# Convolution matmuls of one array half laid between the other half's layer-1 matmuls, and a softmax with its maximum

## The chip, the cores and the metric

The kernel runs on one NeuronCore of a Trainium2 chip. TensorE (PE) multiplies, with a weight load (PEld) in front of each matmul; its results go to PSUM. ScalarE (ACT) and VectorE (DVE) take results out of PSUM, GpSimd (POOL) casts and copies in SBUF, and SyncE (SP) issues nearly all DMAs. The metric is the device time of one execution in microseconds; less is better.

## The reference

`x` is 8 sequences of 4160 tokens with 192 features; `weight` is 8 heads by 7 taps.

```python
w = weight - np.max(weight, axis=-1, keepdims=True)
w = np.exp(w)
w = w / (np.sum(w, axis=-1, keepdims=True) + 1e-09)      # softmax over the 7 taps
x_pad = zeros of 6 rows in front of each sequence, then x
y[b, s, h, g] = sum over k of w[h, k] * x_pad[b, s + k, h, g]   # 24 features per head
h = np.maximum(np.maximum(y @ w1, y @ w2), y @ w3)       # 192 -> 768
out = h @ w_out                                          # 768 -> 192
```

So it is a causal convolution over seven tokens with one filter per head, followed by a feed-forward layer whose hidden value is the largest of three products.

## The kernel before, in words

**Blocks.** The 33280 tokens are cut into 65 blocks of 512 (`NB` is 65). The first four are convolved in a "dense" form (`conv_dense`, L363). The others have their tokens in 32-token pieces on both halves of the partitions and are convolved by `conv` (L341): one block alone, then four pairs, and from block 13 on (`QUADS`) thirteen groups of four. A group of four is convolved in two bursts of four heads each, in the two blocks t = u-4 and t = u-3 before its first block u, where `late` is true. There are thus 26 bursts of four heads.

**The maximum of three.** max(y w1, y w2, y w3) is computed as y w3 + max(relu(y(w1-w3)), y(w2-w3)); `wd` holds the differences, `m16` holds w3 w_out. In each block and for each of six slices j of 128 hidden units, `l1` (L491) makes two sums, `lp` and `lq`, each of three matmuls with 512 columns. `top` (L483) then lets ACT write r = relu(lp) and DVE write h = max(r, lq). `st2` (L533) multiplies h of the block before with `wo` (30 matmuls of 192 columns per half and block, named `po`), and `total` lets ACT and DVE add the halves' sums.

**Two lanes.** Contractions are 64 rows long, so each matmul uses one half of the 128 x 128 array, as a tile of 64 rows by 128 columns: lane 0 is the upper half (`lp`), lane 1 the lower half (`lq`). `mm` (L450) puts a matmul with its column count in a lane's queue, `op` (L454) puts work of other engines behind what was put so far, and `emit` (L461) writes the program: it always takes the next matmul from the lane whose `clock`, the sum of columns so far, is lower. `meet` (L477) empties both lanes and sets the clocks to zero.

**A burst.** In a late block, after `l1(t, 1)` and part of `st2`, `meet()` is called, and then `conv` writes 32 matmuls for four heads (line L354): for each head and each of four 32-token pieces j one on each half, with weights `band` of 39 rows by 32 columns. They are tiles of 64 x 32, so up to eight of them have places of their own in the array (two halves, four column groups). They fill four PSUM tiles G0 to G3, G0 and G2 on the upper half, G1 and G3 on the lower. `evac` (L388) casts them to `ys`, G0 and G2 on ACT, G1 and G3 on DVE. After the second burst `turn` (L398) issues the transposing DMAs from `ys` to `yp` on SP, and `load_on` (L736) issues further loads of `x`. After that the loop goes on with `st2` and `l1(t, 2)`.

**PSUM.** The pool `psp` has two buffers, used in turn by `lp` and G1; `psq` has two, used in turn by `lq` and G3; `psw` has four, for `po`, G0 and G2. A buffer can be written again once its reader (for `lp` the relu, for `lq` the max, for G the cast) is done.

**Start.** The filter's softmax is computed on eight partitions: `Exp` with a running sum on ACT, a reciprocal and a product on DVE (L265 to L271). From its result 38 small matmuls and copies make `band`.

Of the kernel before, what the change touches and what calls it, by code (L numbers as in the profile page):

```python
# [10 lines left out]
FP32 = mybir.dt.float32  # L11
FP16 = mybir.dt.float16
AXX = mybir.AxisListType.X
AF = mybir.ActivationFunctionType

P = 128
KW = 7
PAD = KW - 1
NHEAD = 8
GRP = 24  # L20
# [3 lines left out]
HALF = P // 2  # L24
# [4 lines left out]
def kernel(  # L29
# [12 lines left out]
    nc = tc.nc  # L42
# [15 lines left out]
    for b in range(B):  # L58
        s = nfull * NBLK
        while s < SEQ:  # L60
            n = min(SEQ - s, NBLK - off)
# [27 lines left out]
    TOK = 32  # L89
    NR = NBLK // TOK // 2  # L90
    LAP = PAD + 1
    KR = TOK + LAP
# [6 lines left out]
    const = ctx.enter_context(tc.tile_pool(name="const", bufs=1))  # L99
# [14 lines left out]
    QUADS = 13  # L114
# [58 lines left out]
    for t in range(NDENSE + 1, NB):  # L173
        u = (t - NDENSE - 1) % 2 if t < QUADS else (t - QUADS) % 4
        pairs[t] = (t - u, u, 2 if t < QUADS else 4)

    def place(t):
        return pairs.get(t, (t, 0, 0))

    x16s, slots = {}, {}  # L180
# [48 lines left out]
    wk = const.tile([NHEAD, KW], FP32)  # L229
# [18 lines left out]
    def keep_warm(n, pool=psw, tag="w"):  # L248

        ps = pool.tile([P, NBLK], FP32, tag=tag, name="idle")  # L250
        for _ in range(n):
            nc.tensor.matmul(ps[:], lhsT=idle[:, 0:P], rhs=idle[:], start=True, stop=True)
# [5 lines left out]
    line = const.tile([NHEAD, WIN + 31], FP16)  # L258
# [3 lines left out]
    band = const.tile([P, NHEAD, BAND_W], FP16)  # L262
    nc.vector.memset(band[:], 0.0)
    keep_warm(5, psp, "p")
    wexp = const.tile([NHEAD, KW], FP32)  # L265
    wsum = const.tile([NHEAD, 1], FP32)
    nc.scalar.activation(out=wexp[:], in_=wk[:], func=AF.Exp, accum_out=wsum[:])
    wrec = const.tile([NHEAD, 1], FP32)
    nc.vector.reciprocal(out=wrec[:], in_=wsum[:])
    zero_x(4)  # L270
    nc.vector.tensor_scalar_mul(out=line[:, 31:31 + KW], in0=wexp[:], scalar1=wrec[:])  # L271
    for v in range(2):
        nc.vector.memset(xz[1][v][:], 0.0)
    cast_dense(0, (nc.vector.tensor_copy, nc.vector.tensor_copy))
# [1 line left out]
    for lo, hi, copy in ((0, CUT, nc.scalar.copy), (CUT, WIN, nc.vector.tensor_copy)):  # L276
        bps = psq.tile([32, hi - lo + 3, NHEAD], FP32, tag="q", name=f"band_{lo}")
        for c in range(lo, hi):

            nc.tensor.matmul(bps[:, c - lo:c - lo + 4, :].rearrange("p c h -> p (c h)"),  # L280
                             lhsT=line[:, WIN - 1 - c:WIN + 31 - c],
                             rhs=ident16[0:NHEAD, 0:4 * NHEAD], start=True, stop=True)
        for a in range(4):
            copy(out=band[32 * a:32 * a + 32, :, 32 * a + lo:32 * a + hi],
                 in_=bps[:, 0:hi - lo, :].rearrange("p c h -> p h c"))
# [53 lines left out]
    dense, hs, outs, halves, convs, done = {}, {}, {}, {}, {}, {}  # L339

    def conv(t, pools, heads=range(NHEAD)):  # L341
        if t >= NB:
            return
        t0, _, nu = place(t)
        n = len(pools)
        per = len(heads) * 2 // n
        w = nu * 2 * GRP
        G = [pool.tile([P, per, w], FP32, tag=tag, name=f"G{i}_{t}_{heads[0]}")
             for i, (pool, tag) in enumerate(pools)]
        for k, h in enumerate(heads):  # L350
            for j in range(4):
                for i in range(2):
                    row = slice(HALF * i, HALF * i + KR)
                    nc.tensor.matmul(  # L354
                        G[2 * (k // per) + i][TOK * j:TOK * (j + 1), k % per, :],
                        lhsT=band[row, h, HALF * i + LAP:HALF * i + KR],
                        rhs=x16s[t0][row, h, j, :, :, :].rearrange("p u r c -> p (u r c)"),
                        start=True, stop=True, tile_position=(HALF * i, TOK * j))
        if heads[0] == 0:
            slots[t0] = ysp.tile([P, 2, nu, 2, D], FP16, tag="ys", name=f"ys_{t}")  # L360
        convs[t0] = G, heads[0]

    def conv_dense(t, copies, pools=((None, None),) * 2, order=(0, 1)):  # L363

# [23 lines left out]
    def evac(t, i, copy=nc.scalar.copy):  # L388
        if t >= NB:
            return  # L390
        G, h0 = convs[t]
        per = G[i].shape[1]
        h0 += per * (i // 2)
        copy(out=slots[t][:, i % 2, :, :, GRP * h0:GRP * (h0 + per)].rearrange(  # L394
                 "p u r (h c) -> p h (u r) c", c=GRP),
             in_=G[i][:].rearrange("p h (n c) -> p h n c", c=GRP))

    def turn(t, vs=(0,)):  # L398


        nu = place(t)[2]
        for v in vs:
            n = min(nu, 2)
            yp = ypp.tile([P, 2, 2, n, NC, P], FP16, tag="yp", name=f"yp_{t + v}")
            for u in range(n):
                dense[t + v + u] = yp
            for i in range(2):
                nc.sync.dma_start_transpose(out=yp[:, 0, i, :, :, :].rearrange("p u k n -> p (u k) n"),
                                            in_=slots[t][:, i, v:v + n, :, :].rearrange("p u r d -> p (u r d)"))
# [40 lines left out]
    def mm(i, cols, fn):  # L450
        lanes[i].append((cols, fn))
        put[i] += 1

    def op(fn):  # L454
        ops.append((tuple(put), fn))
# [5 lines left out]
    def emit(rest=False):  # L461


        run_ops()
        while lanes[0] or lanes[1]:
            i = 0 if clock[0] <= clock[1] else 1
            if not lanes[i]:
                if not rest:
                    return
                i = 1 - i  # L470
            cols, fn = lanes[i].popleft()
            fn()
            clock[i] += cols
            gone[i] += 1
            run_ops()
# [15 lines left out]
    def l1(t, j, pools=((psp, "p"), (psq, "q"))):  # L491


        ps = [None, None]

        def product(i, c, n):
            if n == 0:
                pool, tag = pools[i]
                ps[i] = pool.tile([P, NBLK], FP32, tag=tag, name=f"l{tag}{i}_{t}_{j}")
            nc.tensor.matmul(ps[i][:], lhsT=w_of(i, c, j),  # L500
                             rhs=y_all(t, i, c), start=(n == 0), stop=(n == NC - 1))

        for n in range(NC):
            for i in range(2):
                c = n if t >= NDENSE else (i, NC - 1, 1 - i)[n]
                mm(i, NBLK, lambda i=i, c=c, n=n: product(i, c, n))
        op(lambda: top(t, j, ps))
        emit()
# [162 lines left out]
    WPWQ = ((psw, "w"), (psp, "p"), (psw, "w"), (psq, "q"))  # L671
# [64 lines left out]
    def load_on(t):  # L736
        for v in range(loads[t - 1] + 1, loads[t] + 1):
            if v not in loaded:
                load_x(v)
# [4 lines left out]
    for t in range(2, NB):  # L744
        u = convs_at.get(t, NB)
        late = t > 2 and u < NB
        if t in (3, 4):
            double(t + 1)
        if t > 3:
            for v in range(casts.get(t - 1, 8) + 1, casts[t] + 1):  # L750
                cast_x(v)
        l1(t, 0)
        if t == 2:
            first_rest()
        elif t == 3:
            cast_x(8)
            nc.gpsimd.tensor_copy(out=m16[0:HALF, 2, :], in_=m16[HALF:P, 0, :])
            nc.gpsimd.tensor_copy(out=m16[HALF:P, 2, :], in_=m16[HALF:P, 1, :])
        if t > 3 and not late:
            op(lambda t=t: (store(t - 2, 0, 4, (nc.sync,)),  # L760
                            turn(t + 2, (2,)) if place(t + 2)[1:] == (0, 4) else None, load_on(t)))
        else:
            op(lambda t=t: store(t - 2, 0, 4, (nc.sync,)))
        cuts = ROOM if late else EVEN
        st2(t - 1, (cuts[0], cuts[0]))
        for j in range(1, NJ):
            l1(t, j)
            if late and j == 1:
                st2(t - 1, (cuts[0] + OWN + AHEAD, cuts[0] + OWN))
                meet()  # L770
                quad, second = u >= QUADS, u < QUADS or t == u - 3
                conv(u, WPWQ, range(4 * second, 4 * second + 4) if quad else range(NHEAD))
                for i in (0, 2):
                    evac(u, i)
                for i in (1, 3):
                    evac(u, i, nc.vector.tensor_copy)
                if second:
                    turn(u)
                load_on(t)
            if t == 2 and j == 1:  # L780
                meet()
                conv_dense(3, (ACT, DVE))
                zero_x(1, NQ, NR, nc.vector)
                cross(3, GP)
                load_x(8)
                cast_x(6)
            elif t == 2 and j == 3:
                meet()
                conv(u, WW)
                evac(u, 0)  # L790
                evac(u, 1, nc.vector.tensor_copy)
                turn(4)
                load_x(9)
                cast_x(7)
            st2(t - 1, (cuts[j], cuts[j]))
            if j == 1 and t > 4 and t + 2 in pairs and pairs[t + 2][1] % 2 == 0:
                double(t + 2)
            if t == NB - 1 and j == 3:
                op(lambda: store(NB - 2, 0, 2, (nc.sync,)))
        if t == NB - 1:  # L800
            op(lambda: store(NB - 2, 2, 4, (nc.sync,)))
# [29 lines left out]
```

## Time and profile before

| | |
|---|---|
| median of 3 runs | 454.51 us (454.46 to 455.02) |
| profiled execution, first to last instruction (span) | 452.8 us |
| the profiled execution's own time | not listed apart from its span; the median is 1.7 us above the span |
| TensorE busy / weight loads | 446.9 us (99%) / 411.5 us (91%) |
| DVE / ACT / POOL busy | 356.7 us (79%) / 320.0 us (71%) / 203.0 us (45%) |
| mean granted TensorE clock | 0.999 |
| chain that ended last | PE 96%, SP's queue 2%, DMA 1% |
| convolution matmuls (L354), 1152 of them | 17.3 us busy |
| casts of G (L394) | ACT 61, mean 482 ns; DVE 61, mean 550 ns |

In the profile an instruction group is named by line, engine, operation and out<-in. The start of a matmul is recorded; its end is modelled, so a matmul's listed length is longer than the time it holds the array, and the rate is read from the distance between starts. Times on the other engines are starts and lengths in us or ns.

### The profile page before, as it was taken

To read this page: it belongs to the slowest core of one execution; us is meant where nothing else is said; L and a number is where in the kernel's file an instruction comes from. 1 tells how busy PE (TensorE), PEld (TensorE's weight loads), DVE (VectorE), ACT (ScalarE), POOL (GpSimd) and SP (SyncE) were. 2 spreads that over 40 slices of the span, in tenths; PEclk is the share of its full clock that TensorE was granted. 3 is DMA by queue.
4 is the path that set the end of the run, shared out by engine and by line. 5 is a ranking of instruction groups with operands and counts; after the bars stand their busy time and mean duration, and the time that the engine had idled before them with its cause. 6 is when DMAs were issued, how large, how long until landed. Compare 5 with 4: busy or idle time off the path is not lost.

```text
span 452.8 us, 18491 instructions
## 1 busy us (share of the span) xinstructions
PE 446.9 (99%) x7702; PEld 411.5 (91%) x7702; DVE 356.7 (79%) x614; ACT 320.0 (71%) x605; POOL 203.0 (45%) x226
## 2 busy tenths in 40 slices
PE   8999999999999999999999999999999999999997
PEld 4569999999999999999999999999999999999996
DVE  7767778878878788887878788887878788787775
ACT  7767767767777676777767677776767777776664
POOL 2774836556454444635353363444346452504000
PEclk9999999999999999999999999999999999999999
DMA  7978977597966958497585958958594876435223
GB/s 205 231 186 152 225 188 196 143 202 184 171 177 141 178 127 225 123 175 183 119 189 143 192 137 161 199 137 182 135 213 115 178 189 119 116 88 104 59 72 106
DMA packets 127987, 72.03 MB, mean 159 GB/s; under 512 B 52064, under 2 KB 127711, under 8 KB 127903
## 3 DMA queue, kind: packets, MB, share of 16 engines
q1 hardware_dynamic: 127743, 70.75, 69.4%
q8 instruction: 60, 0.98, 1.0%
q14 instruction: 24, 0.20, 0.2%
q10 hardware_dynamic: 160, 0.10, 0.1%
HBM read 33.28 MB, written 25.56 MB: 130 GB/s over the span
## 4 chain that ended last, share of the span: by engine, by line
PE 96%; SPq 2%; DMA 1%; issue 0%; POOL 0%; DVE 0%; POOLq 0%
PE po L564 36%; PE lq L500 31%; PE lp L500 22%; PE G L354 3%; DMA ws<-in_moe_w_dram 1%; PE lw L523 1%; SPq L227 1%; SPq L223 1%; PE D L375 1%; PE po L622 0%; PE po L595 0%; PE lp L523 0%; SPq L164 0%; PE pm L334 0%; POOL wd L299 0%
## 5 line engine op out<-in xcount | busy, mean ns | idle before, releaser
L564 PE MATMUL po<-wo,h 64*128 64x192 f16 x3024 | 331.3, 243 | 0.7 <-issue 0.7
L488 DVE TENSOR_TENSOR h<-r,lq 128x512 f16<-128x512 f16 x384 | 263.0, 686 | 85.9 <-ACT r L487 78.2
L487 ACT ACTIVATE r<-lp 128x512 f16<-128x512 f32 x384 | 229.0, 597 | 115.1 <-PE lp L500 101.8
L500 PE MATMUL lp<-yp,wd 64*128 64x512 f16 x1098 | 295.7, 376 | 0.0
L500 PE MATMUL lq<-yp,wd 64*128 64x512 f16 x1098 | 295.5, 376 | 0.0
L564 PEld LDWEIGHTS <-h 64*128 64x128 f16 x3024 | 241.6, 94 | 6.8 <-issue 4.9
L500 PEld LDWEIGHTS <-wd 64*128 64x128 f16 x2268 | 179.1, 94 | 12.3 <-issue 0.2
L194 POOL CAST x<-xf 103x768 f16<-103x768 f32 x122 | 97.5, 827 | 107.5 <-DMA xf<-in_x_dram 82.0
L564 PE MATMUL po<-m,yp 64*128 64x192 f16 x720 | 141.1, 243 | 0.0
L417 POOL COPY yp<-yp 64x1536 f16<-64x1536 f16 (+1 forms) x62 | 89.6, 1445 | 95.9 <-DMA yp<-ys 70.6
L572 DVE TENSOR_TENSOR o<-a,po 128x384 f32<-128x384 f32 x126 | 69.0, 547 | 0.0
L564 PEld LDWEIGHTS <-yp 64*128 64x128 f16 x720 | 66.3, 94 | 0.3
L571 ACT COPY a<-po 128x384 f32<-128x384 f32 x126 | 59.5, 473 | 0.0
L394 ACT CAST ys<-G 128x384 f16<-128x384 f32 x61 | 26.3, 482 | 9.6 <-PE G L354 9.6
L394 DVE CAST ys<-G 128x384 f16<-128x384 f32 x61 | 31.0, 550 | 0.0
L354 PE MATMUL G<-x,band 39*32 39x192 f16 (+2 forms) x1152 | 17.3, 234 | 0.0
L354 PEld LDWEIGHTS <-band 39*32 39x32 f16 x1152 | 10.7, 91 | 5.2 <-issue 4.7
L500 PE MATMUL lp<-yd,wd 64*128 64x512 f16 x36 | 9.7, 376 | 0.0
L500 PE MATMUL lq<-yd,wd 64*128 64x512 f16 x36 | 9.7, 376 | 0.0
L211 POOL CAST xz<-xf 112x160 f16<-112x160 f32 (+2 forms) x15 | 4.4, 339 | 8.8 <-DVE w3s L303 7.6
L523 PEld LDWEIGHTS <-wd 128*128 128x128 f16 (+1 forms) x48 | 3.0, 96 | 5.6 <-issue 2.2
L375 PEld LDWEIGHTS <-xz 112*32 112x32 f16 x320 | 4.7, 107 | 3.3 <-POOL xz L211 1.3
(72 smaller groups left out, 97.6 us busy)
## 6 DMA issues: line engine op xcount, KB each, us to landing
xf<-in_x_dram SPq DMA_DIRECT2D x113, 234.0 KB
out_dram<-o SPq DMA_DIRECT2D x62, 384.0 KB
xf<-in_x_dram SPq DMA_DIRECT2D x7, 204.8 KB
xf<-in_x_dram SPq DMA_DIRECT2D x3, 420.0 KB
ws<-in_moe_w_dram SPq DMA_DIRECT2D x8, 128.0 KB
yp<-ys SPq DMA_TRANSPOSE x62
out_dram<-o SPq DMA_DIRECT2D x5, 192.0 KB
wos<-in_moe_w_out_dram SPq DMA_DIRECT2D x1, 576.0 KB
```

The costliest lines, as they stand in the source:

```text
L194: nc.gpsimd.tensor_copy(out=x16s[t0][0:K, :, :, u, r, :].rearrange("p h j c -> p j h c"), in_=xf[0:K, 4 * r:4 * r + 4, :].rearrange("p j ( ...
L354: nc.tensor.matmul(G[2 * (k // per) + i][TOK * j:TOK * (j + 1), k % per, :], lhsT=band[row, h, HALF * i + LAP:HALF * i + KR], rhs=x16s[t0] ...
L375: nc.tensor.matmul(ps[32 * g:32 * g + 32, lo:hi], lhsT=xz[t][v][0:rlen, q, 32 * s:32 * s + 32], rhs=band[0:rlen, h, cc:cc + hi - lo], star ...
L394: copy(out=slots[t][:, i % 2, :, :, GRP * h0:GRP * (h0 + per)].rearrange("p u r (h c) -> p h (u r) c", c=GRP), in_=G[i][:].rearrange("p h ...
L417: nc.gpsimd.tensor_copy(out=yp[HALF * i:HALF * (i + 1), 1, :, :, :, :].rearrange("p i u k n -> p (i u k n)"), in_=yp[HALF * (1 - i):HALF * ...
L487: nc.scalar.activation(out=r[:], in_=ps[0][:], func=AF.Relu)
L488: nc.vector.tensor_max(out=hs[t][:, j, :], in0=r[:], in1=ps[1][:])
L500: nc.tensor.matmul(ps[i][:], lhsT=w_of(i, c, j), rhs=y_all(t, i, c), start=(n == 0), stop=(n == NC - 1))
L523: nc.tensor.matmul(open_ps[t, j, i][:], lhsT=a, rhs=b, start=(t, j, i) not in begun, stop=(t, j, i) in begun)
L564: nc.tensor.matmul(ps[b0, i][:, s % 2, :], lhsT=a, rhs=b, start=first, stop=last)
L571: nc.scalar.copy(out=a[:], in_=ps[s - 1, 0][:])
L572: nc.vector.tensor_add(out=outs[t][:, s - 1:s + 1, :], in0=a[:], in1=ps[s - 1, 1][:])
```

## The change

The softmax subtracts the maximum of the seven taps (`reduce_max` with `negate`, given to `Exp` as a bias) and adds 1e-9 to the sum, by an eighth column that a `memset` fills; the sum is a `reduce_sum` on DVE in place of the running sum on ACT.

`conv` is split: `conv_parts` returns the matmuls as a list, and a G tile is taken from its pool when its first matmul is written. For the groups of four, the burst is replaced: after the same `meet()`, the 16 matmuls of the upper half go to lane 0, counted at 48 columns each, then the casts of G0 and G2, then all of `l1(t, 2)` in both lanes, and then the 16 matmuls of the lower half go to lane 1, then the casts of G1 and G3. `emit` mixes them by its clocks. `turn` and `load_on` stand behind these. The single block and the pairs keep their burst.

```diff
-    wexp = const.tile([NHEAD, KW], FP32)
-    wsum = const.tile([NHEAD, 1], FP32)
-    nc.scalar.activation(out=wexp[:], in_=wk[:], func=AF.Exp, accum_out=wsum[:])
+    wexp = const.tile([NHEAD, KW + 1], FP32)
+    nc.vector.memset(wexp[:], 1e-9)
+    wneg = const.tile([NHEAD, 1], FP32)
+    nc.vector.reduce_max(out=wneg[:], in_=wk[:], axis=AXX, negate=True)
+    nc.scalar.activation(out=wexp[:, 0:KW], in_=wk[:], func=AF.Exp, bias=wneg[:])
     wrec = const.tile([NHEAD, 1], FP32)
-    nc.vector.reciprocal(out=wrec[:], in_=wsum[:])
+    nc.vector.reduce_sum(out=wrec[:], in_=wexp[:], axis=AXX)
+    nc.vector.reciprocal(out=wrec[:], in_=wrec[:])
...
+        def product(k, h, j, i):
+            b = 2 * (k // per) + i
+            if G[b] is None:
+                pool, tag = pools[b]
+                G[b] = pool.tile([P, per, w], FP32, tag=tag, name=f"G{b}_{t}_{heads[0]}")
...
+        return [(i, j, lambda k=k, h=h, j=j, i=i: product(k, h, j, i))
+                for k, h in enumerate(heads) for j in range(4) for i in range(2)]
...
         for j in range(1, NJ):
-            l1(t, j)
+            if not (late and u >= QUADS and j == 2):
+                l1(t, j)
             if late and j == 1:
                 st2(t - 1, (cuts[0] + OWN + AHEAD, cuts[0] + OWN))
                 meet()
...
+                if quad:
+                    parts = conv_parts(u, WPWQ, heads)
+                    cols = place(u)[2] * 2 * GRP // 4
+                    for i in range(2):
+                        for a, _, fn in parts:
+                            if a == i:
+                                mm(i, cols, fn)
+                        for b in (i, i + 2):
+                            op(lambda b=b: evac(u, b, (nc.scalar.copy, nc.vector.tensor_copy)[b % 2]))
+                        if i == 0:
+                            l1(t, 2)
+                    emit()
...
                 if second:
-                    turn(u)
-                load_on(t)
+                    op(lambda u=u: turn(u))
+                op(lambda t=t: load_on(t))
+                emit()
```

More of the change, by code (lines that the diff above doesn't have):

```diff
@@ L264 @@
     keep_warm(5, psp, "p")
-    wexp = const.tile([NHEAD, KW], FP32)
-    wsum = const.tile([NHEAD, 1], FP32)
-    nc.scalar.activation(out=wexp[:], in_=wk[:], func=AF.Exp, accum_out=wsum[:])
+    wexp = const.tile([NHEAD, KW + 1], FP32)
[3 more added lines that the diff above has]
+    nc.scalar.activation(out=wexp[:, 0:KW], in_=wk[:], func=AF.Exp, bias=wneg[:])
     wrec = const.tile([NHEAD, 1], FP32)
-    nc.vector.reciprocal(out=wrec[:], in_=wsum[:])
+    nc.vector.reduce_sum(out=wrec[:], in_=wexp[:], axis=AXX)
+    nc.vector.reciprocal(out=wrec[:], in_=wrec[:])
     zero_x(4)
-    nc.vector.tensor_scalar_mul(out=line[:, 31:31 + KW], in0=wexp[:], scalar1=wrec[:])
+    nc.vector.tensor_scalar_mul(out=line[:, 31:31 + KW], in0=wexp[:, 0:KW], scalar1=wrec[:])
     for v in range(2):
@@ L343, in conv, with conv_parts @@
             return
+        for i, j, fn in conv_parts(t, pools, heads):
+            fn()
+    def conv_parts(t, pools, heads):
         t0, _, nu = place(t)
@@ L347, in conv @@
         w = nu * 2 * GRP
[L348 to L358, printed above, removed]
+        G = [None] * n
+        def product(k, h, j, i):
[3 more added lines that the diff above has]
+                G[b] = pool.tile([P, per, w], FP32, tag=tag, name=f"G{b}_{t}_{heads[0]}")
+            row = slice(HALF * i, HALF * i + KR)
+            nc.tensor.matmul(
+                G[b][TOK * j:TOK * (j + 1), k % per, :],
+                lhsT=band[row, h, HALF * i + LAP:HALF * i + KR],
+                rhs=x16s[t0][row, h, j, :, :, :].rearrange("p u r c -> p (u r c)"),
+                start=True, stop=True, tile_position=(HALF * i, TOK * j))
         if heads[0] == 0:
             slots[t0] = ysp.tile([P, 2, nu, 2, D], FP16, tag="ys", name=f"ys_{t}")
-        convs[t0] = G, heads[0]
+        convs[t0] = G, heads[0], per
+        return [(i, j, lambda k=k, h=h, j=j, i=i: product(k, h, j, i))
+                for k, h in enumerate(heads) for j in range(4) for i in range(2)]
     def conv_dense(t, copies, pools=((None, None),) * 2, order=(0, 1)):
@@ L390, in evac @@
             return
-        G, h0 = convs[t]
-        per = G[i].shape[1]
+        G, h0, per = convs[t]
         h0 += per * (i // 2)
@@ L771 @@
                 quad, second = u >= QUADS, u < QUADS or t == u - 3
[L772 to L776, printed above, removed]
+                heads = range(4 * second, 4 * second + 4) if quad else range(NHEAD)
+                if quad:
[10 more added lines that the diff above has]
+                    emit()
+                else:
+                    conv(u, WPWQ, heads)
+                    for i in (0, 2):
+                        evac(u, i)
+                    for i in (1, 3):
+                        evac(u, i, nc.vector.tensor_copy)
                 if second:
-                    turn(u)
-                load_on(t)
+                    op(lambda u=u: turn(u))
+                op(lambda t=t: load_on(t))
+                emit()
             if t == 2 and j == 1:
```

## The prediction

> **What bounds the kernel now.** I read the page's engine shares and chain first, then TensorE's timeline around the bursts.
>
> ```profile
> PE 446.9 (99%) x7702; PEld 411.5 (91%) x7702; DVE 356.7 (79%) x614; ACT 320.0 (71%) x605; POOL 203.0 (45%) x226
> ...
> PE 96%; SPq 2%; DMA 1%; issue 0%; POOL 0%; DVE 0%; POOLq 0%
> ...
> L354 PEld LDWEIGHTS <-band 39*32 39x32 f16 x1152 | 10.7, 91 | 5.2 <-issue 4.7
> ```
>
> TensorE ends the kernel, and from 36 us on it waits for nobody. A plain block has the six-fold rhythm of three 512-column and five 192-column matmuls per lane: 1.06 us, 6.36 us a block. Starts of one lane lie 0.2157 us apart after 512 columns and 0.0825 us after 192, so both lanes stream without holes. The only holes in steady state are beside the convolution: its group of weight loads (L354) has 4.7 us of idle time in front of it, 30 times. One burst, matmuls first, then weight loads:
>
> ```profile
> 137.86 0.41 PE L564 MATMUL po<-wo,h 64*128 64x192 f16 x5
> 138.04 0.24 PE L564 MATMUL po<-m,yp 64*128 64x192 f16 x1
> 138.22 0.52 PE L354 MATMUL G<-x,band 39*32 39x192 f16 x32
> 138.67 0.25 PE L564 MATMUL po<-wo,h 64*128 64x192 f16 x1
> ```
>
> ```profile
> 137.96 0.09 PEld L564 LDWEIGHTS <-yp 64*128 64x128 f16 x1
> 138.21 0.30 PEld L354 LDWEIGHTS <-band 39*32 39x32 f16 x32 [0.16 <-issue]
> 138.67 0.09 PEld L564 LDWEIGHTS <-h 64*128 64x128 f16 x1 [0.16 <-issue]
> ```
>
> The reader should see two gaps, one where tiles of 64x128 give way to 64x32 and one on the way back. In the records' ns the last `po` starts at 138043, the first G at 138216; four rounds of eight G follow, begun at 138216, 138309, 138392 and 138474; the last G starts at 138497, the next `po` at 138672. So a change of tile shape costs 0.173 - 0.0825 = 0.09 us on the way in and 0.175 - 0.0825 = 0.09 us back. The burst takes 0.629 us from last `po` to first `po`: four rounds (0.33) and two changes (0.18) beyond one ordinary step. After a 512-column matmul the change is the same: the last `lq` before the G at 30.26 us starts at 29952, 0.306 us ahead (0.2157 + 0.09). Two bursts in successive blocks (138.29 and 131.35 in the chain) lie 6.94 us apart, 0.58 over a plain block: 26 bursts cost some 15 us, and that is all that the change could touch.
>
> The question is whether one half can take 64x32 tiles while the other streams 64x128. The bursts where the lanes don't end together answer it:
>
> ```profile
> 377.11 0.41 PE L564 MATMUL po<-wo,h 64*128 64x192 f16 x5
> 377.36 0.24 PE L564 MATMUL po<-m,yp 64*128 64x192 f16 x1
> 377.53 0.53 PE L354 MATMUL G<-x,band 39*32 39x192 f16 x32
> ```
>
> Lane 0's seven `po` start in steps of 0.083 us, its last at 377278; lane 1's last (the one with `m`) starts at 377361. The first G belongs to lane 0, stands behind both in the program, and its weights come at 377532: 0.171 us after lane 1's last, 0.254 us after its own. In all 26 bursts of four heads it is 0.170 or 0.171 us after the later lane, whichever the distance of the other (3 to 82 ns). So half 0 waits for half 1 to empty: the tile shape belongs to the whole array.
>
> **The burst's replacement, step by step.** I replayed the writing order by hand with `emit`'s rule (lower clock first, G 48 columns, layer 1 512). After `meet` it runs: 1 G of lane 0; 1 `lq`; 10 G; 1 `lq`; 5 G; `lp`, `lq`, `lp`; 6 G of lane 1; 1 `lp`; 10 G; then `po`. That is ten changes of shape where there were two. With the whole array changing, nothing of the two halves overlaps except in the three-matmul run. G on one half run four abreast, so 1, 10, 5, 6 and 10 take 1, 3, 2, 2 and 3 rounds. Starts, counted from the last `po`: G 0.172; `lq` 0.347 (+0.175); G 0.653 (+0.306); `lq` 0.993 (two rounds 0.165 + 0.175); G 1.299; `lp` 1.557 (0.083 + 0.175); G 2.079 (0.216 + 0.306); `lp` 2.337; G 2.643; `po` 2.983. Before, the same work took 0.629 for the burst and 3 x 0.2157 = 0.647 for `l1(t, 2)`: 1.276. Difference 1.707 us, times 26: **44.4 us** on the path, TensorE being the path.
>
> **A new wait.** G3 is now taken from `psq` after `lq` of j = 2, so `lq` of j = 3 reuses that `lq`'s buffer at once, not one product later. The third `lp` starts at 2.337; relu starts 0.413 us after it (137.317 to 137.73), takes 0.60, max follows 0.03 later and takes 0.69: free at 4.07, 4.13 with 0.06 for the signal (`line` done 3.41, L280 starts 3.47). Lane 1 wants it after nine `po`: 2.983 + 9 x 0.0825 = 3.73. Wait **0.40 us**, times 26 is 10.4 us. The trace has no such wait; its bounds are 0 (if the products come slower than I think, the wait hides) and 0.6 (if the two casts of G, which now follow this max on DVE, 1.01 us, also push the next two max). Behind the waiting matmul everything on TensorE is queued, lane 0's third `lp` first. I take 0.40, since each of its terms is a row.
>
> **What is moved at no cost.** The casts of G0, G2 (ACT, 0.86 for both) end near 2.5, ahead of that relu. The second DMA of `turn`, and behind it on SP `load_on` and the next `store`, wait for G3's cast, at about 5.1 instead of 1.9. The transposes issued at 139.52 feed POOL's copies at 143.80 to 146.79, first read in block u, near 155.7 us by the block rhythm; the loads feed POOL's casts, of which the last that the bursts of the next group (157.9) need ends at 149.47. Both have over 8 us against a delay of 3.2; uncovered, 3.2 us for each of 13 groups would be 42 us.
>
> **Softmax.** DVE is free of `band`'s memset at 2.79. Then a memset (0.12, as `line`'s), `reduce_max` (0.15 to 0.22, the reciprocal's and the product's rows), Exp 0.21, `reduce_sum`, reciprocal, product: `line` at about 4.0 instead of 3.41, 0.6 later; the running sum's read (0.18) goes. That pushes the first convolution and the dense products, but at 14.32 TensorE waits for weights that a DMA landed at 13.37, having been done at 14.00:
>
> ```profile
> 3.01 0.15 DVE L269 RECIPROCAL wrec<-wsum 8x1 f32<-8x1 f32 x1 [0.22 <-ACT wexp L267]
> 3.19 0.22 DVE L271 TENSOR_SCALAR line<-wexp,wrec 8x7 f16<-8x7 f32 x1
> ```
>
> The chain of waits has that matmul:
>
> ```profile
> 13.54 0.74 POOL wd L299
> 14.32 0.39 PE lp L523
> ```
>
> 0.3 of the 0.6 is covered; I take **0.3 us**, bounds 0 and 0.6.
>
> **Sum.** 44.4 + 10.4 + 0.3 = 55.1 us on the profiled span of 452.8 gives 507.9; the runs' median is 1.7 above the span, so 454.5 + 55.1 = **509.6 us**. Own range: 495 (no slot wait, changes a little cheaper) to 519 (wait 0.6, some cast delays).
>
> **The skill on this.** TensorEngine Tiling, Key Properties, says that tiles work independently, different ones loading and multiplying in parallel; read alone that gives the free overlap of the rivals below. It also says that a change of tiling mode, not of tile, drains the array; the rows at 377 us side with that.
>
> **Rivals.**
> 1. The halves keep shapes of their own, and the slot waits. Lane 0: 16 G in four rounds (0.33) and three `lp` (0.647) from 0.083, so `po` at 1.06, 0.216 less than before. But relu then starts after the two casts at 1.34, max ends at 2.65, `lq` of j = 3 wants its slot at 1.80: 0.91 wait. Net +0.69 x 26 = +18: **473 us**. Against it: 377 us. Chance 0.06.
> 2. Faster: the halves keep shapes of their own and `lq`'s slot is free in time, so only the overlap counts: -0.216 x 26 = -5.6, +0.3: **449 us**. It decides from the point where the slot wait is under 0.216 us. For it speaks only that two halves stream side by side within one shape; against it 377 us and the row chain of the slot. Chance 0.03.
> 3. The whole array changes, but TensorE lets lane 0's G pass the waiting `lq`, so that G and products each gather: 16 G, all of `l1`, 16 G, four changes. `po` at 0.172 + 0.2475 + 0.175 + 0.431 + 0.306 + 0.2475 + 0.175 = 1.755, +0.48, and the slot wait 0.32: +0.80 x 26 = +21: **475 us**. The trace shows no matmul that passes one written before it. Chance 0.04. On this the skill's TensorE: Matmul & The Clock Gate (Part 3, The mechanism) holds that matmuls start and end in program order; no row here could show a breach.
> 4. No change of speed, if gains and waits cancel under the first rival: chance 0.01.
>
> **How the numbers follow.** My case has 0.86 and most of it lies in 495 to 519, which leaves out about 2 in 10 with the rivals. A measurement here can tell about 0.2% (0.9 us) from nothing. Slower 0.96, faster 0.03, same 0.01.
>
> **What would show it.** In the changed profile: L354 in five runs per group of four heads, each with about 0.16 us of idle weight load on both sides, some 260 in all; start distances of 0.306 from a lone `lq` to G; `po` 2.98 us after `po`; `lq` of j = 3 waiting for DVE's max about 0.4 us; TensorE still the chain. It is wrong if G and `lq` starts of different halves interleave within 0.1 us, if L354 comes in two runs, or if DVE or SP ends the chain.

## The result, and the profile after

The changed kernel takes 513.57 us (513.27 to 514.16), against 454.49 us for the kernel before beside it: 1.130 times as long, 95% interval 1.128 to 1.132. The profiled execution spans 511.8 us, 59.0 more than before's 452.8.

The page's engine shares and chain, and its two groups for the convolution's weight loads and for layer 1's (line numbers have moved: L363 is the convolution, L511 layer 1, L575 `po`, L498 the relu, L499 the max):

```profile
PE 503.1 (98%) x7702; PEld 399.0 (78%) x7702; DVE 358.0 (70%) x617; ACT 325.4 (64%) x604; POOL 202.8 (40%) x226
...
PE 91%; ACT 4%; DVE 3%; issue 1%; DMA 0%; ACTq 0%
...
L511 PEld LDWEIGHTS <-wd 64*128 64x128 f16 x2268 | 189.8, 94 | 55.0 <-issue 21.0
...
L363 PEld LDWEIGHTS <-band 39*32 39x32 f16 x1152 | 21.2, 91 | 33.9 <-issue 33.4
```

TensorE looks as busy as ever, because a busy share counts a matmul on half the array as a busy engine. The weight loads tell more: their share fell from 91% to 78%, and the idle time ahead of the convolution's rose from 5.2 to 33.9 us. The wait for issue, 33.4 us of it, is put down 134 times, which is five runs of G for each of 26 groups of four heads and one for each of the four pairs.

One group, in TensorE's timeline:

```profile
140.94 0.41 PE L575 MATMUL po<-wo,h 64*128 64x192 f16 x5
141.19 0.24 PE L575 MATMUL po<-m,yp 64*128 64x192 f16 x1
141.36 0.25 PE L363 MATMUL G<-x,band 39*32 39x192 f16 x1
141.55 0.39 PE L511 MATMUL lq<-yp,wd 64*128 64x512 f16 x1
141.86 0.42 PE L363 MATMUL G<-x,band 39*32 39x192 f16 x10
142.22 0.39 PE L511 MATMUL lq<-yp,wd 64*128 64x512 f16 x1
142.53 0.34 PE L363 MATMUL G<-x,band 39*32 39x192 f16 x5
142.80 0.39 PE L511 MATMUL lp<-yp,wd 64*128 64x512 f16 x1
142.81 0.39 PE L511 MATMUL lq<-yp,wd 64*128 64x512 f16 x1
143.03 0.38 PE L511 MATMUL lp<-yp,wd 64*128 64x512 f16 x1
143.34 0.34 PE L363 MATMUL G<-x,band 39*32 39x192 f16 x6
143.61 0.39 PE L511 MATMUL lp<-yp,wd 64*128 64x512 f16 x1
143.92 0.42 PE L363 MATMUL G<-x,band 39*32 39x192 f16 x10
144.28 0.25 PE L575 MATMUL po<-wo,h 64*128 64x192 f16 x1
```

The reader should go down the column of starts. G and layer 1 never start close together: each waits until the other half has finished, and only `lp` and `lq` at 142.80 go side by side. Before, one line of 32 G stood here and the next `po` came 0.63 us after the last; now it comes 3.09 us after.

What then ends the group, in the chain of waits:

```profile
143.68 0.33 PE lp L511
144.01 0.02 issue
144.03 0.61 ACT r L498
144.64 0.02 issue
144.66 0.70 DVE h L499
145.36 0.04 issue
145.40 0.37 PE lq L511
```

The `lq` of the next slice waits for max, which waits for relu, which waits for the last lone `lp`: the 4% of ACT and 3% of DVE in the chain are this. Ahead of this `lq`, at 145.40 us, the weight loads stood idle for 0.35 us.

Two groups in successive blocks lie 9.10 us apart where it was 6.93, and the longer distance over two plain blocks is 21.82 where it was 19.64: 2.17 us for each of 26. Two distances are longer still, 23.12 and 10.41, for TensorE's clock. In these windows the columns are busy time by engine, then granted clock, DMA share and rate:

```profile
87.20:90.20 3.00, 3.00 (x43) 1.09 (x38) 0.69 (x1) 1.33 (x4) 0.00 (x0) 1.00 0.42 131
90.30:93.70 3.40, 3.40 (x33) 2.97 (x33) 2.58 (x5) 1.37 (x3) 0.00 (x0) 0.51 0.36 71
```

Right after a group the clock was half for 3.41 us, and once more from 206.4 us.

### The profile page after: what moved, and what is told of

Read it like the earlier page. It is cut to its first block, busy times and chain, and to the rows that moved or that the text cites. A ratio compares the mean times of both kernels' runs of the same rounds, so it can differ in the third digit from the quotient of the medians.

```text
span 511.8 us, 18467 instructions
## 1 busy us (share of the span) xinstructions
PE 503.1 (98%) x7702; PEld 399.0 (78%) x7702; DVE 358.0 (70%) x617; ACT 325.4 (64%) x604; POOL 202.8 (40%) x226
## 4 chain that ended last, share of the span: by engine, by line
PE 91%; ACT 4%; DVE 3%; issue 1%; DMA 0%; ACTq 0%
PE po L575 32%; PE lq L511 30%; PE lp L511 19%; PE G L363 6%; DVE h L499 3%; ACT r L498 3%; PE lw L534 1%; PE D L387 1%; PE lp L534 0%; PE po L633 0%; PE po L606 0%; ACT xf L137 0%; DMA wk<-in_weight_dram 0%; ACT band L287 0%; ACT L269 0%
## 5 line engine op out<-in xcount | busy, mean ns | idle before, releaser
L499 DVE TENSOR_TENSOR h<-r,lq 128x512 f16<-128x512 f16 x384 | 263.1, 686 | 144.0 <-ACT r L498 138.5
L575 PE MATMUL po<-wo,h 64*128 64x192 f16 x3024 | 339.8, 244 | 0.4 <-issue 0.4
L498 ACT ACTIVATE r<-lp 128x512 f16<-128x512 f32 x384 | 229.0, 597 | 147.0 <-PE lp L511 121.9
L511 PE MATMUL lq<-yp,wd 64*128 64x512 f16 x1098 | 306.4, 378 | 2.6
L511 PE MATMUL lp<-yp,wd 64*128 64x512 f16 x1098 | 306.8, 379 | 0.0
L575 PEld LDWEIGHTS <-h 64*128 64x128 f16 x3024 | 239.4, 94 | 6.7 <-issue 4.7
L511 PEld LDWEIGHTS <-wd 64*128 64x128 f16 x2268 | 189.8, 94 | 55.0 <-issue 21.0
L575 PE MATMUL po<-m,yp 64*128 64x192 f16 x720 | 141.7, 244 | 0.0
L575 PEld LDWEIGHTS <-yp 64*128 64x128 f16 x720 | 66.5, 94 | 0.3
L363 PE MATMUL G<-x,band 39*32 39x192 f16 (+2 forms) x1152 | 49.8, 236 | 0.0
L363 PEld LDWEIGHTS <-band 39*32 39x32 f16 x1152 | 21.2, 91 | 33.9 <-issue 33.4
L405 ACT CAST ys<-G 128x384 f16<-128x384 f32 x61 | 28.8, 479 | 27.9 <-PE G L363 27.9
L511 PE MATMUL lq<-yd,wd 64*128 64x512 f16 x36 | 9.9, 376 | 0.0
L511 PE MATMUL lp<-yd,wd 64*128 64x512 f16 x36 | 9.7, 376 | 0.0
```

The lines of the kernel that those rows point to most:

```text
L363: nc.tensor.matmul(G[b][TOK * j:TOK * (j + 1), k % per, :], lhsT=band[row, h, HALF * i + LAP:HALF * i + KR], rhs=x16s[t0][row, h, j, :, :, ...
L498: nc.scalar.activation(out=r[:], in_=ps[0][:], func=AF.Relu)
L499: nc.vector.tensor_max(out=hs[t][:, j, :], in0=r[:], in1=ps[1][:])
L511: nc.tensor.matmul(ps[i][:], lhsT=w_of(i, c, j), rhs=y_all(t, i, c), start=(n == 0), stop=(n == NC - 1))
L575: nc.tensor.matmul(ps[b0, i][:, s % 2, :], lhsT=a, rhs=b, start=first, stop=last)
```

## The experiments

The theory: the shape of the tiles belongs to the whole array; each change empties it, and a half with the other shape stands meanwhile. The rest is a wait for a PSUM buffer. The rivals: the loss lies in the start; in G running four abreast instead of eight; in mixing two kinds of work in one program order; in late casts, `turn` and loads. All runs here but the exchanged pools and the cut burst shared a chip, where before took 455.08 us.

**The softmax alone.** The kernel before with the new softmax lines.

> The kernel before with the new softmax alone; the bursts stay. Theory (the cost of the change lies in the bursts): 454.6 us, at most 0.3 above before, since in the changed kernel the first burst begins only 0.09 us later than before. Rival (the start carries a part of the 59 us): 455.5 us or more.

Measured 454.99 us, ratio 1.000 (0.998 to 1.002). The start carries nothing that can be measured here; the interval is about 0.8 us to either side.

**G gathered.**

```diff
-                                mm(i, cols, fn)
+                                mm(i, 0, fn)
```

> The changed kernel, with the convolution's matmuls counted at 0 columns in the lanes, so that they are written in one run per half: 16 G of the upper half, all of l1(t, 2) in both lanes, 16 G of the lower half. Same matmuls, but 4 changes of tile shape per group of four heads instead of 10. Theory (each change empties the whole array, 0.10 us, and while one half has its shape the other stands): last po to first po 1.8 us instead of 3.09, a wait of 0.2 for the lq buffer; 20.9 us above before, 475 us (470 to 480). Rival (the loss comes from G running four abreast in one half instead of eight in two, whatever the order): 505 us or more. Rival (late casts, turn and loads): little changed, 505 us or more.

Measured 476.24 us, ratio 1.048 (1.045 to 1.050). TensorE's timeline, two runs of G and the whole of `l1(t, 2)` between:

```profile
135.85 0.24 PE L575 MATMUL po<-m,yp 64*128 64x192 f16 x1
136.03 0.51 PE L363 MATMUL G<-x,band 39*32 39x192 f16 x16
136.47 0.39 PE L511 MATMUL lp<-yp,wd 64*128 64x512 f16 x1
136.47 0.39 PE L511 MATMUL lq<-yp,wd 64*128 64x512 f16 x1
...
137.13 0.24 PE L575 MATMUL po<-wo,h 64*128 64x192 f16 x1
137.30 0.51 PE L363 MATMUL G<-x,band 39*32 39x192 f16 x16
137.74 0.25 PE L575 MATMUL po<-m,yp 64*128 64x192 f16 x1
```

The same 32 G, each half's still alone and four abreast, cost 37 us less, with four changes for ten, and layer 1 has both halves again. From last to first `po` it is 1.89 us where 1.8 was expected and the changed kernel has 3.09; that is 31 of the 37 us. By the steps between starts, about 0.43 us of these 1.20 are two products that no longer run alone, 0.25 three rounds of G, and the other 0.5 six changes. The rest of the 37 is a shorter wait behind the group and no half clock. Running four abreast is no more than the 0.33 us of four extra rounds in this (9 us of the 21 over before); late casts and `turn`, still behind all of it, are not the 59 us either.

**The lower half first.**

```diff
-                    for i in range(2):
+                    for i in (1, 0):
...
-                        if i == 0:
+                        if i == 1:
                             l1(t, 2)
```

> The changed kernel with the lower half's convolution before l1(t, 2) and the upper half's after it. By the lanes' clocks a lone lp then comes right after po, so there are 8 changes of shape, and lp ends well before lq, so that relu is done when lq ends and the lq buffer comes back in time. Theory with the buffer wait of 0.36 us: 39 us above before, 494 us (490 to 498), no wait of lq for DVE. Rival (changes count, but the wait for the buffer is hidden anyway): two changes and one round of G less, 0.29 x 26 = 7.5 us below the changed kernel, 506 us.

Measured 500.35 us, ratio 1.102 (1.099 to 1.104): between the two expectations, 6 us above the theory's. `lq` waits no more, but the chain shows another:

```profile
140.67 0.20 PE G L363 x2
140.88 0.02 issue
140.90 0.49 ACT ys L405
141.39 0.04 issue
141.43 0.34 PE po L575 x4
```

ACT's cast of G0, now late, holds a buffer of `psw`, and `po` of the third quarter wants it. The wait for `lq` was gone and one for `po` had come; groups lie 8.68 us apart.

**The lower half first, with the pools of G exchanged.** G1 and G3, now early, take the buffers of `psw`, and G0 and G2, now late, those of `psp` and `psq`.

```diff
+    PWQW = ((psp, "p"), (psw, "w"), (psq, "q"), (psw, "w"))
...
-                    parts = conv_parts(u, WPWQ, heads)
+                    parts = conv_parts(u, PWQW, heads)
```

> The kernel with the lower half first, with the PSUM pools of the G tiles exchanged: G1 and G3 (now first) in psw, G0 and G2 (now last) in psp and psq. In the run with the lower half first, po of the third quarter waited at 141.43 us for ACT's cast of G0, which was in psw, 0.24 us per group of four heads (its burst cost 1.75 us over before where 1.52 was expected). Theory (eight changes at 0.11 us, halves apart, and the rest is a wait for whichever buffer comes back last): with the pools exchanged no matmul waits, 26 x 0.24 = 6.1 us less than with the lower half first, 494.2 us (492.5 to 496). Rival (the 6 us are something else, late casts in general or the order of the lanes): 500.4 us. Exchanging the pools may also bring a new wait of lp or lq, which would show as DVE or ACT in the chain and leave the time above 496.

Measured 493.98 us beside 454.99 of before, ratio 1.087 (1.084 to 1.089). The chain goes from G to `po` with nothing between:

```profile
138.31 0.32 PE lq L511
138.63 0.35 PE G L363 x10
138.98 0.52 PE po L575 x10
```

Groups now lie 8.45 us apart, 1.52 over before: what eight changes and the lone half come to when no buffer is waited for. So the wait for `po` was a wait for a buffer and a cost of its own, 0.23 us a group (8.68 less 8.45). The wait for `lq` in the changed kernel, 0.35 us, was not taken out by itself in any run; it is read from the chain there and is gone in both runs with the lower half first.

**One shape.** G as 64x128 tiles of 48 columns; this leaves out three quarters of the convolution's columns.

```diff
-                G[b][TOK * j:TOK * (j + 1), k % per, :],
-                lhsT=band[row, h, HALF * i + LAP:HALF * i + KR],
-                rhs=x16s[t0][row, h, j, :, :, :].rearrange("p u r c -> p (u r c)"),
-                start=True, stop=True, tile_position=(HALF * i, TOK * j))
+                G[b][:, k % per, 48 * j:48 * j + 48],
+                lhsT=band[row, h, 0:P],
+                rhs=x16s[t0][row, h, j, 0, :, :].rearrange("p r c -> p (r c)"),
+                start=True, stop=True, tile_position=(HALF * i, 0))
```

> The changed kernel in its own order, but the groups of four are convolved with tiles of 64x128 and 48 columns in place of 64x32 and 192: as many matmuls, about the same time on the lane (16 x 0.0225 us against four rounds of 0.0825), no change of shape. It leaves out three quarters of the columns and writes all 128 rows, so its values are not the convolution. Theory (only the change of shape keeps the halves apart): both halves stream side by side, last po to first po about 1.1 us, and then the waits for the lp and lq buffers of 0.4 each decide: 18 us above before, 473 us (466 to 478). Rival (mixing the two kinds of work in one program order is what costs): 505 us or more. Rival that the waits for buffers are not there: 449 us.

Measured 470.77 us, ratio 1.036 (1.034 to 1.038). TensorE's timeline shows what the change wanted:

```profile
141.15 0.38 PE L518 MATMUL lq<-yp,wd 64*128 64x512 f16 x1
141.15 0.38 PE L364 MATMUL G<-x,band 39*128 39x48 f16 x9
141.37 0.38 PE L518 MATMUL lq<-yp,wd 64*128 64x512 f16 x1
141.38 0.25 PE L364 MATMUL G<-x,band 39*128 39x48 f16 x4
141.48 0.37 PE L518 MATMUL lp<-yp,wd 64*128 64x512 f16 x1
```

Nine G run on the upper half under one `lq` of the lower. Mixing in one program order costs next to nothing as long as the shape stays: from last to first `po` it is 1.19 us, where 1.1 was expected and before has 1.28 for the same work. Still groups lie 7.57 us apart where before has 6.93, because the group is then short and the casts, relu and max can't follow: the chain has ACT at 9% and DVE at 7%, with a cast, relu and max ahead of the next `lq`. So, as far as this run can stand for independent halves, even they would not have made this order pay.

**The burst of before, cut in two.**

```diff
         for k, h in enumerate(heads):
+            if between and k == 2:
+                between()      # one po of each lane: st2(t - 1, (13, 9))
             for j in range(4):
```

> The kernel before, with its burst cut in two: after the first two heads one po of each lane is written, then the other two heads. Same matmuls, two more changes of tile shape per group of four heads and nothing else, both halves together throughout. Theory (about 0.10 us for each change): 26 x 0.20 = 5.3 us above before, 459.8 us (458.8 to 460.8). Rival (a change by itself is free, only a half that stands alone costs): 454.5 us.

Measured 460.86 us beside 454.36, ratio 1.013 (1.010 to 1.015), at the upper end of what was expected.

```profile
135.18 0.36 PE L356 MATMUL G<-x,band 39*32 39x192 f16 x16
135.47 0.25 PE L566 MATMUL po<-wo,h 64*128 64x192 f16 x1
135.48 0.25 PE L566 MATMUL po<-m,yp 64*128 64x192 f16 x1
135.66 0.36 PE L356 MATMUL G<-x,band 39*32 39x192 f16 x16
```

Groups lie 7.15 us apart instead of 6.93, and 19.87 instead of 19.64: 0.22 and 0.23 us more. Both halves always work together here, so this is the price of two changes by themselves, 0.11 us each, or 5.9 us for 52. The remaining 0.6 us of the medians is inside the scatter of this run (459.07 to 463.31).

## Why the prediction was right, and the terms that were off

The forecast was 509.6 us, slower at 0.96, range 495 to 519; 513.57 came. The order of runs of G and layer 1, the whole-array shape, the new `lq` wait and TensorE as the path all stand in the profile as foretold. By terms, against the spans' 59.0 us:

| step | forecast | measured | from |
|---|---|---|---|
| ten changes and lone halves | 44.4 | 47.1 | (3.090 - 0.630 - 0.647) x 26 |
| wait for the `lq` buffer | 10.4 | 9.2 | (2.166 - 1.813) x 26 |
| softmax | 0.3 | 0.1 | first group 0.09 us later, 78.228 for 78.140 |
| half clock, twice | 0 | 2.6 | 23.12 - 21.82 and 10.41 - 9.10 |
| sum | 55.1 | 59.0 | |

That the result lies well inside the range is in part luck: the room above the sum was meant for a longer wait and late casts, and a clock drop that has no term in it used part of it.

*Price of a change.* 0.09 us was the gap alone. The first round on a half after a change also takes 0.010 us longer: the prediction's own four rounds started 93, 83 and 82 ns apart, and it went on with 82.5. Nine such rounds lie between the two `po`, and each of these nine steps is 9 to 15 ns longer than forecast (from a lone `lq` to the next G 0.317 us, where 0.306 was forecast): together the 0.107 us by which 3.090 exceeds 2.983. The cut burst gives the whole price, 0.11. The Trainium skill's TensorEngine Tiling (Key Properties) has the drain at a change of mode; the runs with 2, 4, 8 and 10 changes agree that it is paid each time, 0.10 to 0.13 us when rounds and products are taken off the distance from `po` to `po`. One of the signs had a number off: the weight loads' idle time ahead of a run of G is 0.16 us behind `po`, as forecast, but 0.23 or 0.42 behind a product.

*The wait.* It was the chain that was forecast (lone `lp`, relu, max, `lq`), 0.35 in place of 0.40 us. That such a wait is a cost of its own is shown by the exchanged pools for `po`; for `lq` it rests on the chain. Groups are no farther apart than these two terms make them, so nothing more was pushed by the casts behind it.

*Softmax.* `line` was 0.98 us later, not 0.6, yet only 0.09 remained at the first group. That is one execution of each, and the softmax alone shows 0.28 there with no time lost over the kernel, so the 0.1 is within the start's scatter. The step that was missed is below.

*The clock* had no term. It is the one part of the 59 us without a cause: each of the runs of the changed kernel has a mean clock of 0.993, where one in 13 of before and one in six of the cut burst went down to 0.996, so two drops belong to this program, but 24 of 26 like groups pass without one.

*The rivals* fell where they should. Of the two with halves of their own shape, the one-shape run is the nearest to the world they need, and it gave 470.8 us, close to the first one's 473: the row chain that spoke for the buffer wait in them was right too. The gathered order reached by writing it so cost 476 us, which is the third rival's 475; TensorE did not gather by itself.

## What to carry to other kernels

Before laying tiles of two shapes beside each other, look in the trace for a place where the two lanes end apart and see which one the first matmul of the new shape waits for; that single distance decided this prediction. Count runs of a shape, not matmuls: at 0.11 us a change, gathering each half's 16 G here was worth more (476 us) than laying them between the other half's products (514 us), and the burst that fills both halves in one shape was the best of all (454 us). And when a tile takes a PSUM buffer at a new place in the order, follow the ring: here removing one wait put the next on another pool.

## What was not expected of the hardware

**A table load behind the wait for an input.** ACT's timeline, one line of before and two of the changed kernel:

```profile
1.38 1.28 ACT L267 ACT_TABLE_LOAD   x1 [1.38 <-PEq L815]
...
2.17 1.28 ACT L269 ACT_TABLE_LOAD   x1 [2.17 <-DMA wk<-in_weight_dram]
3.47 0.30 ACT L269 ACTIVATE wexp<-wk,wneg 8x7 f32<-8x7 f32 x1
```

Before, ACT's table load for `Exp` began at 1.38 us without waiting for `wk`; now it waits for `wk` and begins at 2.17, and in the run with the softmax alone at 2.15. In the new form the wait for the input stands ahead of the table load; whether for the bias or for the running sum that went, no run tells apart. `wneg` was ready at 2.87 us, but `Exp` began at 3.47, behind the table load, and took 0.30 us instead of 0.21: that is the 0.4 us by which `line` was later than forecast.

**Half a clock with a busy engine.** The two drops lasted 3.41 us at 0.5, while TensorE was 98% busy by the page. The Trainium skill's TensorE: Matmul & The Clock Gate (Part 1) has the same window of 3413 ns, which runs on freely, and the two clocks, with idleness as the cause. The runs agree with length and ratio; no idle stretch of that length is in the trace, but just ahead of the first drop, from 87.2 to 90.2 us, weight loads were busy for only 1.09 of 3.00 us.

Where a group falls in time matters. By the profile's records the clock rose at 8.42 us, fell at 90.34, rose at 93.75, fell at 206.39 and rose at 209.80 us: 24, 1, 33 and 1 steps of 3.413 us. On this grid only three of the 26 groups lie whole, from `po` to `po`, inside one step, those whose G begin at 87.32, 203.19 and 213.59 us, and the clock fell at the end of the first two. So none of the 23 that straddle a step's end brought a drop. Why the third passed is open; weight loads were busy for as little of its step as of the other two, 1.4 of 3.41 us.

That many changes of shape look like idleness to the clock's gate is a guess that no run here tested; neither run with eight changes shows a drop in its profile. And a drop is not special to lone halves: the cut burst's profile has one from 30.15 to 33.57 us, six steps after the clock rose, and it began when TensorE had stood without a matmul for 2.0 us of a wait of 2.17.
